# Second layer of the last MLP: seven block products for two token tiles instead of eight

## The chip, the cores and the metric

One core of a Trainium2 chip runs the program. Its engines are PE (TensorE, matrix products), DVE (VectorE), ACT (ScalarE), POOL (GpSimd) and SP, which here only issues DMAs. Each engine takes its instructions in program order; they wait for one another by semaphores. The metric is the device time of one execution in microseconds, the median of the runs shown; less is better.

## The reference, cut to what matters

Packed attention and a gated MLP give `x` of 4608 tokens with 512 features (the `y` of the kernel). The last part is

```
a = x @ w1            # 512 -> 1024
b = x @ w2            # 512 -> 1024
h = a * b @ w3        # 1024 -> 1024
out = h @ w_out       # 1024 -> 512
```

Everything is float32. The weights come as pairs of 32-bit words (64-bit floats) and are converted on the chip.

## The kernel before, in words

Tokens are cut into nine tiles of 512 (`TT`, `NTILE`). A float32 product is made of three fast ones: each operand is split into `hi` (ACT copies it into the reduced format, line 55) and `lo` (DVE or POOL subtracts, line 56), and PE adds hi·hi, hi·lo and lo·hi in one PSUM bank.

After the attention and the gate layer, the program goes through these stages:

- **`y_part(t)`** (line 538) makes `y` of one tile: 12 units, one for each row block `kk` of the hidden layer, of 12 matmuls each. `fetch_h` loads the row of a unit four units ahead into one of five buffers `hr`, `split_h` splits it two units ahead (three buffers `hh` and `hl`). At the end `y` is split into `y_h` and `y_l` and both go to DRAM three units later (`store_later`); tile 8 stays in SBUF.
- **`folded(half)`** (line 595) multiplies `w3` and `w_out` into `w34`, which goes to DRAM.
- **Conversion.** `converting` (line 116) loads a weight block of 512 KB some jobs ahead (`load64`), and `convert` needs two ACT, two DVE and one POOL instruction for it. `together` (line 405) takes steps of such generators between the units of the main one. The three calls at lines 613 to 616 are three `y` tiles with `folded(0)`, two with `folded(1)`, and the tiles 5, 6 and 7 with the last 15 jobs (the blocks of `w1` and `w2`, split into `w12_h`, `w12_l`, which stay in SBUF). `y_part(8)` comes last, with `last_loads`, which loads and splits `w34` in eight steps.
- **The layer itself**, tile by tile, in eight steps `i` of 128 features each. `ab_part(t, i)` (line 641) does two times 12 matmuls of 512 columns, for `a` and `b` in a PSUM bank each. ACT copies `a`, DVE multiplies by `b`, and the product is split. `out_part(t, i)` (line 659) does 12 matmuls into the four banks of the tile's output, one step later, so that PE has the next `ab_part` while the product is made. `fetch_y` loads the tile after next.

All DMAs are issued by SP in program order. A tile's buffers rotate: a load into a buffer waits until the last reader of its old content is done.

Of the kernel before, what the change touches and what calls it, by code (L numbers as in the profile page):

```python
# [32 lines left out]
def packed_attention_swiglu_bilinear(ctx: ExitStack, tc, qT, kT, v, pT, rms_g, w_gv, w_out,  # L33
# [11 lines left out]
    yh_d = dram.tile([NT // TT, 128, 4, TT], F32, name="yh_d")  # L45
    yl_d = dram.tile([NT // TT, 128, 4, TT], F32, name="yl_d")
# [69 lines left out]
    def converting(jobs, take):  # L116


        ahead = [load64(src) for src, *_ in jobs[:AHEAD64]]
        yield  # L120
        for i, job in enumerate(jobs):
            take(ahead.pop(0), *job[1:])
            if i + AHEAD64 < len(jobs):
                ahead.append(load64(jobs[i + AHEAD64][0]))
            yield
# [4 lines left out]
    def as_f32(w):  # L130
        o = cv_of[0].tile([128, 512], F32, tag="c_o", name="c_o", bufs=2)
# [3 lines left out]
    converted = set()  # L135

# [7 lines left out]
    AHEAD64 = 3  # L144
# [334 lines left out]
    wp = ctx.enter_context(tc.tile_pool(name="wo", bufs=1, side="left"))  # L479
# [57 lines left out]

    def y_part(t, tag):
# [13 lines left out]
        h = yp.tile([128, 4, TT], F32R, tag="y_h", name="y_h", bufs=2)  # L552
        l = yp.tile([128, 4, TT], F32R, tag="y_l", name="y_l", bufs=2)
        for m in range(4):
            split(h[:, m], l[:, m], acc[m], nc.vector)
        if t + 1 < NTILE:
            store_later(3, out=yh_d[t], in_=h.bitcast(F32))
            store_later(3, out=yl_d[t], in_=l.bitcast(F32))
        else:
            yt[t] = h, l  # L560
# [16 lines left out]

    jobs = []
# [16 lines left out]
    def folded(half, tag):  # L595
        acc = four(tag)
        ready(16 + 8 * half)
        for j in range(8):
# [16 lines left out]
    together(chained(y_part(3, "at"), y_part(4, "gv"), folded(1, "at")), 32.0, (8, some(late, 8), 0.0, 0.7))
    together(chained(y_part(5, "gv"), y_part(6, "at"), y_part(7, "gv")), 36.0, (15, late, 0.0, 0.95))
    split(*behind.pop(), nc.vector)
# [106 lines left out]
```

## Time and profile before

| | |
|---|---|
| time, median of 3 runs | 1469.1 us (1468.96 to 1470.85) |
| profiled execution: time, span of its core | 1469.47 us, 1467.7 us |
| PE busy | 1401.5 us, 95% of the span |
| DVE, ACT, POOL busy | 642.8, 539.7, 329.6 us |
| moved by DMA | 180.23 MB, mean 123 GB/s |
| PE waits after the start of the `y` stage | 1.4 us in all, both in `y_part(8)` |

PE is busy almost all the time, and from the `y` stage on it hardly waits. The other engines and the DMA queues have room on the average, least in the stage of the `y` tiles.

### The profile page before, as it was taken

What the parts mean: (1) busy time and instruction counts of PE and PEld (TensorE: products, weight loads), DVE (VectorE), ACT (ScalarE), POOL (GpSimd) and SP (SyncE); (2) the same over time, 40 slices, a digit from 0 to 9 for tenths busy, and PEclk for the clock granted to TensorE, in tenths of its full rate; (3) what the DMA queues carried; (4) which work ended last, traced back from release to release, by engine and by line L of the source; (5) the groups of instructions that cost most, each with busy time, mean ns of one, the idle gap of its engine ahead of it and who ended that gap; (6) DMA issues with size and microseconds to landing.
All of it is one profiled execution on the core that took longest, in us unless ns stands there. A gap on an engine that the chain in (4) does not pass through costs nothing.

```text
span 1467.7 us, 22283 instructions
## 1 busy us (share of the span) xinstructions
PE 1401.5 (95%) x8872; PEld 1150.7 (78%) x8872; DVE 642.8 (44%) x1088; ACT 539.7 (37%) x1079; POOL 329.6 (22%) x332
## 2 busy tenths in 40 slices
PE   3679999999999899999999999999999999999998
PEld 1468778778788788888888878888888888888887
DVE  4787576666666457726266531111111121111111
ACT  2455555555555555535255431111111111111111
POOL 2456445445445542201012220000000000000000
PEclk7599999999999999999999999999999999999999
DMA  9754453454222466746357620202020210202000
GB/s 303 279 203 126 155 181 115 148 162 139 79 88 88 160 240 238 250 172 213 132 186 262 232 94 0 86 1 87 0 86 0 87 60 27 86 1 86 0 29 29
DMA packets 59608, 180.23 MB, mean 123 GB/s; under 512 B 6768, under 2 KB 6768, under 8 KB 52720
## 3 DMA queue, kind: packets, MB, share of 16 engines
q1 hardware_dynamic: 59504, 178.81, 35.1%
q8 instruction: 69, 1.13, 0.3%
q14 instruction: 35, 0.29, 0.1%
HBM read 119.02 MB, written 59.77 MB: 122 GB/s over the span
## 4 chain that ended last, share of the span: by engine, by line
PE 85%; DVE 6%; ACT 3%; DMA 3%; issue 2%; POOL 0%; SPq 0%; ACTq 0%; DVEq 0%; POOLq 0%
PE gv L648 27%; PE gv L374 16%; PE at L663 14%; PE at L547 10%; PE gv L547 9%; PE at L335 2%; DMA w<-in_w_gv_dram 2%; PE at L601 1%; PE gv L601 1%; PE at L290 1%; DVE th L381 1%; DVE a L272 1%; PE at L206 1%; DVE wbl L56 1%; DVE wgv L112 1%
## 5 line engine op out<-in xcount | busy, mean ns | idle before, releaser
L653 DVE TENSOR_TENSOR hr<-hr,gv 128x512 f32<-128x512 f32 x72 | 49.5, 687 | 422.4 <-PE gv L648 422.4
L56 DVE TENSOR_TENSOR hl<-hr,hh 128x512 fp32r<-128x512 f32 x180 | 153.3, 855 | 182.7 <-ACT hh L55 162.8
L55 ACT ACTIVATE hh<-hr 128x512 fp32r<-128x512 f32 x180 | 112.8, 630 | 306.4 <-DVE hr L653 208.9
L386 POOL TENSOR_TENSOR ht<-th,vl 128x288 f32<-128x288 f32 x192 | 163.8, 861 | 178.4 <-ACT vl L385 97.7
L374 PE MATMUL gv<-ah,wbh 128*128 128x288 f32 x768 | 179.4, 315 | 16.0 <-ACT vl L385 12.5
L374 PEld LDWEIGHTS gv<-ah,wbh 128*128 128x128 f32 x768 | 123.3, 191 | 67.5 <-issue 26.9
L374 PE MATMUL gv<-al,wbh 128*128 128x288 f32 x768 | 167.3, 298 | 0.0
L374 PE MATMUL gv<-ah,wbl 128*128 128x288 f32 x768 | 165.6, 297 | 0.0
L648 PE MATMUL gv<-y_h,w_h 128*128 128x512 f32 x576 | 155.6, 392 | 0.0
L648 PE MATMUL gv<-y_l,w_h 128*128 128x512 f32 x576 | 155.4, 391 | 0.0
L648 PE MATMUL gv<-y_h,w_l 128*128 128x512 f32 x576 | 154.8, 391 | 0.0
L652 ACT ACTIVATE hr<-gv 128x512 f32<-128x512 f32 x72 | 43.1, 598 | 274.6 <-PE gv L648 274.6
L114 POOL TENSOR_TENSOR c_o<-c_o,c_y 128x512 int32<-128x512 int32 x52 | 73.1, 1406 | 248.8 <-DVE c_o L112 245.0
L648 PEld LDWEIGHTS gv<-y_l,w_h 128*128 128x128 f32 x576 | 108.1, 188 | 23.8
L648 PEld LDWEIGHTS gv<-y_h,w_h 128*128 128x128 f32 x576 | 108.1, 188 | 23.7
L648 PEld LDWEIGHTS gv<-y_h,w_l 128*128 128x128 f32 x576 | 108.1, 188 | 23.3
L374 PEld LDWEIGHTS gv<-al,wbh 128*128 128x128 f32 x768 | 125.4, 191 | 1.1 <-DVE al L56 0.6
L374 PEld LDWEIGHTS gv<-ah,wbl 128*128 128x128 f32 x768 | 124.8, 190 | 0.0
L663 PE MATMUL at<-w_h,hl 128*128 128x512 f32 x288 | 113.6, 395 | 0.0
L663 PE MATMUL at<-w_l,hh 128*128 128x512 f32 x288 | 113.3, 393 | 0.0
L663 PE MATMUL at<-w_h,hh 128*128 128x512 f32 x288 | 112.0, 389 | 0.0
L381 DVE SCALAR_TENSOR_TENSOR th<-th,gv 128x288 f32<-128x288 f32 x192 | 84.2, 444 | 63.1 <-ACT th L380 62.1
(112 smaller groups left out, 2158.1 us busy)
## 6 DMA issues: line engine op xcount, KB each, us to landing
hT_d<-ht SPq DMA_DIRECT2D x96, 288.0 KB, 2.5
hr<-hT_d SPq DMA_DIRECT2D x108, 256.0 KB, 4.1
w<-in_w_gv_dram SPq DMA_DIRECT2D x24, 512.0 KB, 7.8
w<-in_w_out_dram SPq DMA_DIRECT2D x20, 512.0 KB, 4.5
v<-in_v_dram SPq DMA_DIRECT2D x8, 1152.0 KB, 7.5
q<-in_qT_dram SPq DMA_DIRECT2D x8, 1152.0 KB, 6.9
out_dram<-hr SPq DMA_DIRECT2D x36, 256.0 KB, 2.1
w<-in_w3T_dram SPq DMA_DIRECT2D x16, 512.0 KB, 4.8
```

Source lines behind the costliest of these rows:

```text
L55: nc.scalar.activation(out=hi, in_=src, func=AF.Copy)
L56: eng_lo.tensor_tensor(out=lo, in0=src, in1=hi.bitcast(F32), op=ALU.subtract)
L114: nc.gpsimd.tensor_tensor(out=d, in0=d, in1=shape(y), op=ALU.add)
L335: nc.tensor.matmul(t[32 * c:32 * c + 32, e, :], lhsT=gP1T[64 * e:64 * e + 64, c, :], rhs=wgv[64 * e:64 * e + 64, c, :, 256 * g:256 * g + 256],
L374: nc.tensor.matmul(t[:, :HALF], lhsT=w[:, e, 256 * i + 128 * f:256 * i + 128 * f + 128], rhs=x[:, e, HALF * hf:HALF * hf + HALF], start=(n ...
L381: nc.vector.scalar_tensor_tensor(out=th, in0=th, scalar=1.0, in1=t[:, :HALF], op0=ALU.add, op1=ALU.mult)
L386: nc.gpsimd.tensor_tensor(out=ht[:, hf], in0=th, in1=vl, op=ALU.mult)
L547: nc.tensor.matmul(acc[m], lhsT=w[:, kk, 128 * m:128 * m + 128], rhs=x, start=(kk == 0 and a == 0), stop=(kk == NF - 1 and a == 2))
L648: nc.tensor.matmul(p[j], lhsT=w[:, kk, j, 128 * i:128 * i + 128], rhs=x[:, kk], start=(n == 0), stop=(n == 11))
L652: nc.scalar.activation(out=a, in_=p[0], func=AF.Copy)
L653: nc.vector.tensor_tensor(out=a, in0=a, in1=p[1], op=ALU.mult)
L663: nc.tensor.matmul(acc[m], lhsT=x[:, 128 * m:128 * m + 128], rhs=w[:, i], start=(i == 0 and n == 0), stop=(i == 7 and n == 2))
```

## The change

The second layer is taken for two tiles at a time, as a product of 2 by 2 blocks. The rows of `w1` and `w2` are halved (256 input features each), `w1` and `w2` are the two block rows of the result, and the two token tiles are its two block columns. Seven products of sums of blocks replace the eight products of blocks: `prod(bank, j, start)` is one of them, six matmuls (three fast products for each of two row blocks). Some of them are added on top of a bank whose earlier content an engine has read before.

- `layer2` converts the 16 weight blocks in four groups of four and `group` makes seven sums of each group, split into hi and lo (POOL and DVE; ACT for hi), in one of two SBUF tiles `stage`. They go to DRAM as `ws_d`, four stores of 917 KB for each group.
- `y` of a tile goes to DRAM unsplit, once (`y_d`, 1 MB instead of two times 1 MB); tile 8 too.
- For each pair of tiles `fetch_y` loads both `y`, and `sums` makes seven sums of their blocks and splits them (`xh`, `xl`, one buffer each). In each of the eight steps of a pair `load_w` loads the block sums of the next step from `ws_d`, 1.835 MB, into one of two buffers.
- The first tile's output is added up during the steps (`acc1`), the second tile's behind them (`acc2`), from its kept products `n2_h` and `n2_l`; the next pair's `sums` lie in that part.
- Tile 8 has no partner and is taken as two halves of 256 tokens.
- `w34` is split half in `y_part(8)`, half in the first four steps of the first pair (`rest`), where the load and the split of a row stand directly behind each other.

```diff
-    AHEAD64 = 3
+    ahead64 = [3]
...
+    stage = [p2.tile([128, 8192], F32R, name=f"stage{i}") for i in range(2)]
+    ahead64[0] = 2
+    c_o_bufs[0] = 4
...
-            split(h[:, m], l[:, m], acc[m], nc.vector)
-        if t + 1 < NTILE:
-            store_later(3, out=yh_d[t], in_=h.bitcast(F32))
-            store_later(3, out=yl_d[t], in_=l.bitcast(F32))
+            evict(y[:, m], acc[m], m)
+        store_later(3, out=y_d[t], in_=y)
...
+        put(3, a22, nc.vector)
+        nc.gpsimd.tensor_tensor(out=a22, in0=a21, in1=a22, op=ALU.add)
+        put(0, a11, nc.vector)
+        nc.gpsimd.tensor_tensor(out=a21, in0=a11, in1=a21, op=ALU.subtract)
+        yield
+        nc.gpsimd.tensor_tensor(out=a11, in0=a22, in1=a11, op=ALU.subtract)
+        put(1, a12, nc.vector)
+        put(4, a22, nc.vector)
+        yield
...
+        put(2, a12, nc.vector)
+        for i in range(4):
+            store_later(2 + i, out=ws_d[4 * c + i, :, r], in_=to[:, i].bitcast(F32))
...
-    together(chained(y_part(5, "gv"), y_part(6, "at"), y_part(7, "gv")), 36.0, (15, late, 0.0, 0.95))
+    together(chained(y_part(5, "gv"), y_part(6, "at"), y_part(7, "gv")), 36.0, (33, layer2(), 0.0, 0.97))
+    flush()
+    p2_ctx.close()
...
+    wt = ctx.enter_context(tc.tile_pool(name="wt", bufs=1, side="right"))
...
+    def load_w(n):
+        if n < 8 * len(pairs):
+            w = wt.tile([128, 2, 7, 2, 128], F32R, tag="w", name="w", bufs=2)
+            nc.sync.dma_start(out=w.bitcast(F32), in_=ws_d[n % 8])
...
+        put(0, b11, nc.vector)
+        yield
+        diff(b11, b12, b11)
+        put(4, b11, nc.vector)
+        yield
...
     fetch_y(0)
-    together(y_part(NTILE - 1, "at"), 12.0, (8, last_loads(), 0.0, 0.9))
+    load_w(0)
+    together(y_part(NTILE - 1, "at"), 12.0, (8, sums(0), 0.0, 0.85), (4, last_loads(0), 0.1, 0.9))
...
+        for i in range(8):
+            wi = ws.pop(8 * p + i)
+            load_w(8 * p + i + 1)
+            if i == 0:
+                fetch_y(p + 1)
+            ta, tb, tc_ = (bank()[:, :w] for _ in range(3))
...
+            prod(ta, 0, True)
+            nc.scalar.activation(out=p1, in_=ta, func=AF.Copy)
+            if second:
+                second()
+            prod(tb, 5, True)
+            dve(u2, tb, p1, ALU.add)
+            prod(tc_, 4, True)
+            prod(ta, 1, False)
+            prod(tb, 6, False)
+            u3 = tmp()[:, :w]
+            dve(u3, tb, p1, ALU.add)
+            dve(c22, tc_, u3, ALU.add)
+            if i > 0:
+                if i == 1:
+                    acc1 = four("at")
+                outs(acc1, i - 1, *n1.pop(i - 1), ms)
+            prod(tb, 3, False)
+            c21 = tmp()[:, :w]
+            dve(c21, tb, p1, ALU.add)
+            dve(c21, c21, ta, ALU.mult)
+            prod(tc_, 2, False)
+            dve(u2, tc_, u2, ALU.add)
+            nc.gpsimd.tensor_tensor(out=u2, in0=u2, in1=c22, op=ALU.mult)
...
+            split(hi[:, :w], lo[:, :w], c21, nc.vector)
...
+            if p == 0:
+                next(rest, None)
...
+        outs(acc2, 0, n2_h[:, 0], n2_l[:, 0], ms)
+        outs(acc1, 7, *n1.pop(7), ms)
+        for m in ms:
+            store(rows[0], acc1, m)
+        ahead = sums(p + 1)
...
+        for m in ms:
+            outs(acc2, 7, n2_h[:, 7], n2_l[:, 7], (m,))
+            store(rows[1], acc2, m)
```

What moves is seen best in the order of the instructions at three places. The first is PE in the layer itself. Before, one step of a tile: two banks `gv` of 12 matmuls each, and the beginning of the 12 matmuls of `out_part`.

```order
L648 MATMUL gv_12169<-y_h_11730,w12_h_6924 128x512 x4
L648 MATMUL gv_12169<-y_l_11731,w12_h_6924 128x512 x4
L648 MATMUL gv_12169<-y_h_11730,w12_l_6925 128x512 x4
L648 MATMUL gv_12170<-y_h_11730,w12_h_6924 128x512 x4
L648 MATMUL gv_12170<-y_l_11731,w12_h_6924 128x512 x4
L648 MATMUL gv_12170<-y_h_11730,w12_l_6925 128x512 x4
L663 MATMUL at_12106<-w34_h_9524,hh_12153 128x512
L663 MATMUL at_12106<-w34_l_9525,hh_12153 128x512
```

After, step 0 of the first pair, from its third product on: 9806 is the bank `tc_`, 9804 is `ta`, 9805 is `tb`.

```order
L799 MATMUL gv_9806<-xh_9560,w_9538 128x512 x2
L799 MATMUL gv_9806<-xl_9561,w_9538 128x512 x2
L799 MATMUL gv_9806<-xh_9560,w_9538 128x512 x2
L799 MATMUL gv_9804<-xh_9560,w_9538 128x512 x2
L799 MATMUL gv_9804<-xl_9561,w_9538 128x512 x2
L799 MATMUL gv_9804<-xh_9560,w_9538 128x512 x2
L799 MATMUL gv_9805<-xh_9560,w_9538 128x512 x2
L799 MATMUL gv_9805<-xl_9561,w_9538 128x512 x2
L799 MATMUL gv_9805<-xh_9560,w_9538 128x512 x4
L799 MATMUL gv_9805<-xl_9561,w_9538 128x512 x2
L799 MATMUL gv_9805<-xh_9560,w_9538 128x512 x2
L799 MATMUL gv_9806<-xh_9560,w_9538 128x512 x2
```

A product is six matmuls, and a bank comes back after one or two other products. In step 0 the products 6 and 3 stand directly behind each other in `tb` (the `x4` are the last two matmuls of the one and the first two of the other); in the other steps 12 matmuls of `outs` stand between them.

The second place is SP's queue where `y_part(7)` ends and `y_part(8)` begins (`hr<-hT_d` is a row for a unit, `hr<-w_d` a row of `w34`). Before:

```order
L485 DMA hr<-hT_d 128x512 [waits DMAHW7_49,DMAHW2_49,DVE_49]
L485 DMA hr<-hT_d 128x512 [waits DMAHW3_49,DVE_49]
L631 DMA y_h<-yh_d 128x2048
L632 DMA y_l<-yl_d 128x2048
L485 DMA hr<-hT_d 128x512 [waits DMAHW4_49,DVE_49]
L485 DMA hr<-w_d 128x512 [waits DMAHW5_49,DVE_49]
L485 DMA hr<-hT_d 128x512 [waits DMAHW6_49,DVE_49]
L485 DMA hr<-w_d 128x512 [waits DMAHW7_49,DVE_49]
L485 DMA hr<-hT_d 128x512 [waits DMAHW4_49,Pool_49]
L354 DMA yh_d<-y_h 128x2048 [waits DMAHW0_49]
L354 DMA yl_d<-y_l 128x2048 [waits DMAHW1_49]
```

After:

```order
L497 DMA hr<-hT_d 128x512 [waits DMAHW1_49,DVE_49]
L356 DMA ws_d<-stage_6939 128x1792 [waits DMAHW0_49,DVE_49]
L356 DMA ws_d<-stage_6939 128x1792
L356 DMA ws_d<-stage_6939 128x1792 [waits DMAHW2_49]
L356 DMA ws_d<-stage_6939 128x1792 [waits DMAHW3_49]
L356 DMA y_d<-y 128x2048 [waits DMAHW4_49,DVE_49,Activation_49]
L694 DMA yi<-y_d 128x2048 [waits DMAHW5_49]
L694 DMA yi<-y_d 128x2048 [waits DMAHW6_49]
L703 DMA w<-ws_d 128x3584 [waits DMAHW2_49,DMAHW1_49,DMAHW3_49,DMAHW0_49,DMAHW7_49,PE_49,Pool_49]
L497 DMA hr<-hT_d 128x512 x3
L497 DMA hr<-w_d 128x512 [waits DVE_49]
```

Between the row for the last unit that is loaded in `y_part(7)` and the next three rows there now stand the last group's four stores of block sums, the store of `y` of tile 7, two loads of `y` and the first load of block sums, which waits for the four stores (its buffer lies where `stage` lay). Before, two loads of `y` stood there.

The third place is SP's queue at the start of the first pair, after the last row of `y_part(8)`:

```order
L356 DMA y_d<-y 128x2048 [waits DVE_49]
L703 DMA w<-ws_d 128x3584
L694 DMA yi<-y_d 128x2048 [waits DMAHW6_49]
L694 DMA yi<-y_d 128x2048 [waits Pool_49]
L497 DMA hr<-w_d 128x512 [waits DMAHW1_49,DMAHW0_49]
L703 DMA w<-ws_d 128x3584 [waits PE_49]
```

The row of `w34` that the first step of `rest` loads and splits at once stands behind 5 MB of other transfers.

## Rows read from the trace of the kernel before

**Rows 1.** The page: busy time, share of the span and instructions of each engine.
```profile
PE 1401.5 (95%) x8872; PEld 1150.7 (78%) x8872; DVE 642.8 (44%) x1088; ACT 539.7 (37%) x1079; POOL 329.6 (22%) x332
```

**Rows 2.** The page: the chain that ended last, by engine.
```profile
PE 85%; DVE 6%; ACT 3%; DMA 3%; issue 2%; POOL 0%; SPq 0%; ACTq 0%; DVEq 0%; POOLq 0%
```

**Rows 3.** Stretches: busy time and count of each engine, granted clock, DMA share, GB/s.
```profile
900.00:1440.00 540.00, 540.00 (x2355) 441.72 (x2354) 100.00 (x146) 89.91 (x147) 0.00 (x0) 1.00 0.12 43
760.00:830.00 70.00, 70.00 (x310) 57.96 (x310) 47.57 (x67) 39.06 (x67) 15.96 (x11) 1.00 0.65 221
```

**Rows 4.** Groups of the second layer (868 to 1467): busy us, mean ns, idle before.
```profile
L648 PE MATMUL gv<-y_h,w_h 128*128 128x512 f32 x576 | 155.6, 392 | 0.0
L663 PE MATMUL at<-w_h,hl 128*128 128x512 f32 x288 | 113.6, 395 | 0.0
...
L653 DVE TENSOR_TENSOR hr<-hr,gv 128x512 f32<-128x512 f32 x72 | 49.5, 687 | 422.4 <-PE gv L648 422.4
L55 ACT ACTIVATE hh<-hr 128x512 fp32r<-128x512 f32 x72 | 45.5, 632 | 208.9 <-DVE hr L653 208.9
```

**Rows 5.** Timeline of PE: first and last matmuls of the second layer.
```profile
868.55 1.09 PE L648 MATMUL gv<-y_h,w_h 128*128 128x512 f32 x4
...
1462.94 0.39 PE L663 MATMUL at<-w_h,hl 128*128 128x512 f32 x1
```

**Rows 6.** Timeline of PE in the gate layer, matmuls of 288 columns.
```profile
299.83 0.43 PE L374 MATMUL gv<-al,wbh 128*128 128x288 f32 x2
...
300.90 0.42 PE L374 MATMUL gv<-ah,wbl 128*128 128x288 f32 x2
```

**Rows 7.** Timeline in the second layer: end of a bank's matmuls, and its reader.
```profile
1206.25 1.07 PE L648 MATMUL gv<-y_h,w_l 128*128 128x512 f32 x4
...
1207.36 0.60 ACT L652 ACTIVATE hr<-gv 128x512 f32<-128x512 f32 x1 [2.11 <-PE gv L648]
```

**Rows 8.** DMA issues: KB each, median us from issue to landing.
```profile
y_h<-yh_d SPq DMA_DIRECT2D x8, 1024.0 KB, 5.0
y_l<-yl_d SPq DMA_DIRECT2D x8, 1024.0 KB, 7.0
...
hr<-w_d SPq DMA_DIRECT2D x8, 256.0 KB, 3.0
```

**Rows 9.** Stretches with little but stores, mixed traffic, and loads (columns as before).
```profile
750.00:755.00 5.00, 5.00 (x24) 4.14 (x23) 3.53 (x6) 2.73 (x5) 1.28 (x1) 1.00 0.66 212
775.00:780.00 5.00, 5.00 (x24) 4.13 (x23) 3.77 (x7) 3.57 (x7) 1.59 (x1) 1.00 1.02 417
...
1206.40:1214.00 7.60, 7.60 (x35) 6.23 (x34) 1.38 (x2) 1.23 (x2) 0.00 (x0) 1.00 0.90 336
```

**Rows 10.** Timeline in `y_part(8)`, with the issues of SP.
```profile
839.49 1.12 SPq L485 DMA_DIRECT2D hr<-w_d  x1
...
847.03 0.63 ACT L55 ACTIVATE w_h<-hr 128x512 fp32r<-128x512 f32 x1 [6.72 <-DMA hr<-w_d]
...
848.24 0.50 PE L547 MATMUL at<-hh,wo_h 128*128 128x512 f32 x1 [0.54 <-ACT hh L55]
...
849.62 0.50 PE L547 MATMUL at<-hl,wo_h 128*128 128x512 f32 x1 [0.88 <-DVE hl L56]
```

**Rows 11.** Timeline in `y_part(8)`: a POOL and a DVE instruction at one time.
```profile
852.51 1.29 POOL L56 TENSOR_TENSOR w_l<-hr,w_h 128x512 fp32r<-128x512 f32 x1 [3.50 <-ACT w_h L55]
...
852.99 1.37 DVE L56 TENSOR_TENSOR hl<-hr,hh 128x512 fp32r<-128x512 f32 x1 [2.82 <-ACT hh L55]
```

**Rows 12.** Stretches around waits of PE (columns as before).
```profile
10.00:12.00 2.00, 0.00 (x0) 0.00 (x0) 1.35 (x4) 1.34 (x2) 0.00 (x0) 1.00 1.20 391
12.00:14.00 2.00, 1.08 (x6) 1.06 (x7) 0.00 (x0) 2.00 (x6) 0.00 (x0) 0.69 1.03 252
14.00:16.00 2.00, 1.69 (x8) 1.21 (x6) 1.74 (x4) 2.00 (x5) 0.61 (x1) 0.50 0.95 221
...
845.00:850.00 5.00, 3.58 (x15) 2.41 (x15) 1.78 (x2) 1.67 (x3) 1.28 (x1) 1.00 0.51 185
```

More of the change, by code (lines that the diff above doesn't have):

```diff
@@ L135, in packed_attention_swiglu_bilinear @@
     converted = set()
+    c_o_bufs = [2]
     def gv_weight(w, g, c):
@@ L611, in folded, with last_split @@
         yield 1.0
+    def last_split():
+        split(*behind.pop(), nc.vector)
+        staged.append(0)
+        yield
     together(chained(y_part(0, "at"), y_part(1, "gv"), y_part(2, "at"), folded(0, "gv")), 44.0,
              (18, some(late, 18), 0.0, 0.78))
-    together(chained(y_part(3, "at"), y_part(4, "gv"), folded(1, "at")), 32.0, (8, some(late, 8), 0.0, 0.7))
-    together(chained(y_part(5, "gv"), y_part(6, "at"), y_part(7, "gv")), 36.0, (15, late, 0.0, 0.95))
-    split(*behind.pop(), nc.vector)
@@ L618, in packed_attention_swiglu_bilinear @@
-    cv2_ctx.close()
-    wq = ctx.enter_context(tc.tile_pool(name="w34", bufs=1, side="left"))
-    w34_h = wq.tile([128, 8, DM], F32R, name="w34_h")
-    w34_l = wq.tile([128, 8, DM], F32R, name="w34_l")
-    def last_loads():
-        for kk in range(8):
-            split(w34_h[:, kk], w34_l[:, kk], fetch(w34_d[128 * kk:128 * kk + 128, :]), nc.gpsimd)
-            yield
-    def fetch_y(t):
-        h = yp.tile([128, 4, TT], F32R, tag="y_h", name="y_h", bufs=2)
-        l = yp.tile([128, 4, TT], F32R, tag="y_l", name="y_l", bufs=2)
-        nc.sync.dma_start(out=h.bitcast(F32), in_=yh_d[t])
-        nc.sync.dma_start(out=l.bitcast(F32), in_=yl_d[t])
-        yt[t] = h, l
+    late = chained(late, last_split())
@@ L659, in out_part, with tmp @@
-    def out_part(t, i, acc, ms=range(4)):
-        hi, lo = abt[t, i]
+    wo_ctx.close()
+    p3 = ctx.enter_context(tc.tile_pool(name="p3", bufs=1, side="left"))
+    n2_h = p3.tile([128, 8, TT], F32R, name="n2_h")
+    n2_l = p3.tile([128, 8, TT], F32R, name="n2_l")
+    for kk in range(4, 8):
+        w34_h[kk] = p3.tile([128, DM], F32R, name=f"w34_h{kk}")
+        w34_l[kk] = p3.tile([128, DM], F32R, name=f"w34_l{kk}")
+    rest = last_loads(1)
+    def tmp(tag="hr", bufs=5):
+        return (rot if tag == "hr" else p3).tile([128, TT], F32, tag=tag, name=tag, bufs=bufs)
@@ L693, in packed_attention_swiglu_bilinear @@
+    for p in range(len(pairs)):
+        run(p)
     man.close()
```

216 lines of the change are left out of this document (143 added, 73 removed).

## The prediction

> **What bounds the kernel now.** I read the page first: PE is busy for 95% of the span [rows 1] and makes 85% of the chain that ended last [rows 2], so time comes off where PE does less or waits less. Then stretches, to get what one matmul costs. In the second layer 540 us hold 2355 matmuls of 512 columns, **0.2293 us each**; in the `y` stage 70 us hold 310, 0.226 us each, or 2.71 us for a unit of 12 [rows 3]. PE is busy for the whole of both. The layer's matmuls begin at 868.55 and the last one starts at 1462.94 and takes 0.39 [rows 5], which is 594.8 us; 9 tiles x 8 steps x 36 matmuls x 0.2293 give 594.3. No matmul group of the layer has idle time before it [rows 4]. Nothing but the number and the width of matmuls sets this stage. DVE is 68% busy in the `y` stage (47.57 of 70 us) and 19% in the layer (100 of 540), and the DMA share is 0.65 and 0.12 [rows 3]: the work that the change adds lies partly where there is less room.
>
> **What the change takes away.** A pair needs 8 steps x 7 products x 6 matmuls + 2 x 8 x 12 of the output = 528 matmuls of 512 columns for 576. Four pairs: 2112 x 0.2293 = 484.3 us. Tile 8, in halves, needs 336 matmuls of 256 columns and 96 of 512. The narrow ones have no row; 288 columns take (300.90 - 299.83) / 8 = 0.134 us [rows 6], and the 224 columns up to 512 make 0.0955, so 32 fewer than 288 make about 0.120. That is 40.3 + 22.0 = 62.3. Together 546.6 for 594.3: **-47.7 us**. (Bounds of the narrow ones: 0.115 if the whole pitch scaled with columns, 0.134 if it didn't fall any more; -2 to +5 us.)
>
> **Banks that come back.** A product that is added on top must wait until DVE or ACT has read the bank. A reader starts when the last matmul ends, and PE could have gone on 0.39 - 0.23 = 0.16 earlier; with the 0.04 between an end (1207.32) and its reader (1207.36) [rows 7] and 0.69 for the DVE instruction [rows 4], the bank is free about 0.9 us after its product. Between most uses lie one or two products of 1.38 us, or 12 output matmuls of 2.75 us, and that covers it. Step 0 has no output matmuls between the products 6 and 3: 0.95 us in four pairs, 0.55 at half width: **+4.4**. If the cover of the other 35 steps were gone it would cost 35 x 0.95 = 33 us; DVE has 7 such instructions, 4.8 us, in a step of 12.4 (9.6 if all took the 1.37 us that one takes beside POOL [rows 11]), so it isn't.
>
> **The boundary before `y_part(8)`.** First what transfers cost. The two 1.05 MB loads of `y` land 5.0 and 7.0 us after issues that lie 0.4 apart [rows 8], and that stretch moves 336 GB/s at a share of 0.90, 0.373 MB/us at full share; stores go at 417 / 1.02, 0.41; mixed small traffic at 212 / 0.66, 0.32 [rows 9]. A lone 0.26 MB lands after 3.0 [rows 8], 2.3 of it not data. A queue is served in order: the row of `w34` issued at 839.49, behind the stores of `y`, reaches ACT at 847.03, and PE waits 0.54 + 0.88 us for the row split behind it [rows 10]. Now count from T, where PE would start `y_part(8)`. The last block sum is made two units before, T - 5.7. Four stores, 3.67 MB from T - 4.5 on: until T + 4.4. The store of `y`: until T + 7. Two loads of `y`: T + 12.6. The first block sums: T + 17.5. Only then the row for the fifth unit, issued behind all that, lands near T + 19; ACT 0.63 [rows 4] and DVE 0.69 later, at T + 20.2, it can be used, where PE is through with four units at T + 10.8. ACT also sits on the first `sums` until T + 11, which splits the fourth unit's row late, but that lies inside the same wait. 9.3 us, and 0.9 for DVE, whose `sums` (difference, split, difference) fill more than a unit afterwards, less the 1.4 us that the same place costs now: **+8.8**. PE then stands still twice for some 4 us. At the start, where PE has nothing to do at 10 to 12 and little after it, the granted clock is 0.69 and then 0.50 of full speed (0.50 is 1.2 of 2.4 GHz); after the 1.4 us of this place now it stays 1.00 [rows 12]. Four us as at 12 to 16 cost 1.6 us a wait, so 0 to 3.2; I take **+2**.
>
> A rule of the Trainium skill speaks against the change here, in "TensorE: Matmul & The Clock Gate", section "HAM oscillation — how this bites in real kernels": gaps of PE bring the clock down and the work behind each gap begins slow. By the first rows above that is 3.2, by the last 0.
>
> **The first pair.** The store of `y` of tile 8, the second block sums and two loads of `y` are 1.05, 1.83 and 2.1 MB; from about 2 us after the pair's start they run until 4.5, 9.4 and 15.0, and the row of `w34` behind them lands at 16.5. ACT waits for it, at the end of step 0; the copy of step 1's first bank is done at 17.8, and PE wants that bank at 14.7 (10.6 + three products): **+3.3**. The next rows are issued a step ahead of their use.
>
> **The stream of block sums.** 1.835 MB take 2.3 + 1.835 / 0.373 = 7.2 us from issue. A buffer comes free at the start of a step, so a full step of 54 x 0.2293 = 12.4 us hides it. In step 0 it is issued 1.5 us late, behind the last output stores, and lands at about 9.2, before 9.6 + 0.95. The half tiles have steps of 42 x 0.120 + 6 x 0.2293 = 6.4: 0.8 late six times, and 9.2 - 5.6 = 3.6 at the first: **+8.4**.
>
> By the Trainium skill, "DMA: Bandwidth & Descriptors", section "Anatomy of one DMA — SWDGE (gpsimd) path", a DMA costs 2.0 us and 1 us for each 436 KB; this load would take an estimated 6.2 us, less than the half step, and the sum would be some 6 us lower. The page fits another issuing path, and the stretch of loads above is slower than its rate, so the sum stays with the rows.
>
> **The units with block sums** (`y_part(5)` to `(7)`). DMA time by the rates above: 36 rows 29.5, 16 blocks of weights 26, three `y` 7.7, the 12 stores that fall in 27, together 90 of 97.6 us. Where a row, a block and a store fall in one unit, 0.8 + 1.6 + 2.2 stand against 2.7; unit by unit the backlog grows to about 9 us, three quarters through group 2's conversion. A row is asked for some four units before its split is due and six before PE, so this hides. DVE goes from 68% to some 88%: 13 more splits net of the `y` halves (about 9 us more) and POOL's 16 additions of 1.29, which slow what runs beside them [rows 11]. Cover is the two units that a split is ahead, 5.4 us. Bounds 0 and 16 (1 us in each of the 16 units of a group); near the small end, since PE has no wait at all there now: **+2**. The unsplit `y`, `last_split` and the two-ahead loads: nothing, hidden in ACT and DVE time that falls.
>
> **Sum:** -47.7 + 4.4 + 8.8 + 2 + 3.3 + 8.4 + 2 = -18.8. The profiled execution took 1469.47 (span 1467.7 and 1.8 around it), 0.4 over the median: about **1450 us**. The layer would take some 563 us and `y_part(8)` some 11 us more than its 32.5.
>
> **Rivals.**
> - *Transfers are quicker than I reckon.* The second load of `y` lands 2.0 us after the first, issued 0.4 later: 0.43 MB/us [rows 8]. Then half steps lack 0.2 us, the first 3, the boundary shrinks by 2, the first pair by 1.5, no clock is lost and the `y` units lose nothing: 12 us less, 1439. Against it is the stretch's mean rate [rows 9].
> - *DVE becomes the bound in the units with block sums.* For it: 68% now, 88% worked out, an in-order engine that waits for ACT and POOL within each group. A us in each group unit gives 1465. Against it: four units of a group are followed by four of conversion, which have less.
> - *Slower: the block sums come too slowly.* The lowest rate at a nearly full share is 221 / 0.95 = 0.23 MB/us [rows 12]. A load then takes 10.2 us: the half tile loses 21 more, each pair's first step 1.6, the boundary 6, and the time is 1484. From about 0.27 MB/us down the change costs more than it saves. For it: each pair's first loads run beside output stores and loads of `y`; against it: the rows of `y`, 8 KB long in each partition, went at 0.373, and these are 14 KB.
> - That PE doesn't do less can't be: the instructions are counted.
>
> **How the numbers follow.** The forecast has 0.52, quicker transfers 0.22, DVE 0.13, slow block sums 0.08, and 0.05 stays for something else at either side. Faster (by over 0.2%, 2.9 us, about what can be told from no change): the first two, most of the third and some of the rest, 0.85; the same 0.06; slower 0.09. The range reaches to the quick case and to the DVE case: 1436 to 1466.
>
> **What would show it.** 1344 matmuls of 512 and 336 of 256 columns at line 799, the first at 0.229 each; idle PE time of about 1 us in step 0 of each pair, released by DVE; one wait of 4 us or more, twice, in `y_part(8)`, released by ACT or DVE behind a row that came by DMA; a wait for ACT in step 1 of the first pair; waits for the load of block sums in the half tile alone. It is wrong if block sums hold PE in full steps, if the `y` units show waits of more than 5 us in all, or if `y_part(8)` takes under 36 us.

## The result, and the profile after

| | before | after |
|---|---|---|
| time, median of 4 runs | 1469.26 us | **1453.72 us** (1451.48 to 1457.4) |
| profiled execution: time, span | 1469.47, 1467.7 us | 1451.91, 1450.1 us |
| PE busy | 1401.5 us | 1360.0 us |

The ratio is 0.9895, 95% interval 0.987 to 0.9919: faster by about 1%, 3.7 us above the forecast time and well inside the range. The page of the changed kernel, first its busy times, then its chain by engine and by line, for [rows 1, 2]:

```profile
PE 1360.0 (94%) x8824; PEld 1121.8 (77%) x8824; DVE 795.9 (55%) x1267; ACT 546.7 (38%) x1080; POOL 489.9 (34%) x438
...
PE 75%; DVE 8%; DMA 5%; ACT 3%; issue 3%; POOL 1%; SPq 1%; ACTq 0%; DVEq 0%; POOLq 0%
PE gv L799 22%; PE gv L376 17%; PE at L566 8%; PE gv L772 7%; PE at L772 7%; PE gv L566 6%; PE at L337 2%; DMA hr<-w_d 2%; DMA w<-ws_d 2%; PE at L657 2%; PE gv L657 2%; DVE stage L56 1%; PE at L292 1%; DVE c_t L111 1%; DVE th L383 1%
```

PE is still the bound, and two DMAs with 2% each are now among the first lines of the chain, which weren't there before: the rows of `w34` and the loads of block sums. DVE and POOL are busy for 153 and 160 us more than before.

Stretches of the changed kernel (columns as in [rows 3]): the second layer, the `y` units with block sums, and three places behind waits of PE.

```profile
900.00:1370.00 470.00, 466.46 (x2033) 382.77 (x2034) 201.40 (x267) 93.34 (x140) 120.00 (x75) 1.00 0.40 148
760.00:830.00 70.00, 67.53 (x296) 55.29 (x297) 59.34 (x73) 41.10 (x72) 36.92 (x24) 1.00 0.94 349
...
1383.00:1393.00 10.00, 9.81 (x64) 9.56 (x65) 3.42 (x8) 1.75 (x5) 1.47 (x2) 0.83 0.49 182
850.00:855.00 5.00, 1.99 (x4) 1.29 (x5) 2.96 (x3) 1.66 (x3) 0.00 (x0) 0.58 1.04 441
...
901.00:906.00 5.00, 4.81 (x14) 3.86 (x15) 0.86 (x2) 0.66 (x2) 2.25 (x2) 0.66 0.37 153
```

The layer is dense: PE is idle for 3.5 of 470 us. In the `y` units it was busy for the whole 70 us before; now it lacks 2.5 us there, DVE has gone from 47.57 to 59.34 us and the DMA share from 0.65 to 0.94. In the last three rows the granted clock is below 1.00.

What PE waited for from the start of the `y` tiles to the end (total us, times, longest):

```profile
PE at L566 <- ACT hh L55: 7.3, 2, 6.7
PE gv L799 <- DMA w<-ws_d: 6.1, 4, 2.8
PE gv L799 <- DVE hr L767: 3.6, 5, 0.8
PE gv L799 <- ACT hr L805: 3.6, 1, 3.6
PE gv L566 <- DVE hl L56: 2.3, 3, 1.2
PE at L566 <- DVE hl L56: 2.1, 3, 1.3
```

25 us in all, for 1.4 before. Line by line: `y_part(8)`, the stream of block sums in the half tiles, the banks of step 0, the first pair, and in the last two lines the splits of the `y` units (3.6 us in `y_part(5)` to `(7)`, 0.8 in `y_part(8)`).

The stages, from the timeline of PE. What lies ahead of the first `y` tile is the same program in all kernels here, yet that tile begins at 527.4 to 532.1 us in them, so stages are compared and not ends:

| us | before | after | by |
|---|---|---|---|
| tiles 0 to 4 and `folded` twice | 207.52 | 206.92 | -0.6 |
| `y_part(5)` to `(7)` | 97.96 | 102.79 | +4.8 |
| `y_part(8)` | 34.61 | 44.78 | +10.2 |
| second layer | 594.78 | 564.06 | -30.7 |
| ahead of it all and behind it | | | -1.3 |

First and last matmul of the layer, for [rows 5] (the first and the last line). The two lines between are for [rows 6]: the first of 42 matmuls of 256 columns without a wait, and the matmul of 512 columns that follows them.

```profile
882.22 0.63 PE L799 MATMUL gv<-xh,w 128*128 128x512 f32 x2
...
1425.89 0.40 PE L799 MATMUL gv<-xh,w 128*128 128x256 f32 x2
...
1430.92 0.39 PE L772 MATMUL at<-w_h,hh 128*128 128x512 f32 x1
...
1445.89 0.39 PE L772 MATMUL gv<-w_h,n_l 128*128 128x512 f32 x1
```

42 narrow matmuls take 1430.92 - 1425.89 = 5.03 us, 0.120 each.

**The boundary**, for [rows 10]: the timeline of SP's issues, ACT and PE around the start of `y_part(8)` at 837.44.

```profile
834.44 3.01 SPq L356 DMA_DIRECT2D ws_d<-stage  x4
838.40 0.36 SPq L356 DMA_DIRECT2D y_d<-y  x1
838.80 2.54 SPq L694 DMA_DIRECT2D yi<-y_d  x2
844.78 0.32 SPq L703 DMA_DIRECT2D w<-ws_d  x1
845.15 2.10 SPq L497 DMA_DIRECT2D hr<-hT_d  x3
...
850.83 1.06 ACT L55 ACTIVATE xh<-yi 128x1024 fp32r<-128x1024 f32 x1 [12.56 <-DMA yi<-y_d]
851.80 0.61 ACT L55 ACTIVATE hh<-hr 128x512 fp32r<-128x512 f32 x1
...
858.32 0.63 ACT L55 ACTIVATE hh<-hr 128x512 fp32r<-128x512 f32 x1 [2.35 <-DMA hr<-hT_d]
...
852.46 0.80 PE L566 MATMUL at<-hh,wo_h 128*128 128x512 f32 x1 [6.70 <-ACT hh L55]
...
859.00 0.50 PE L566 MATMUL at<-hh,wo_h 128*128 128x512 f32 x1 [0.64 <-ACT hh L55]
```

Read from the last but one upwards: PE waits 6.70 us for the split of the fourth unit's row. ACT makes that split at 851.80, directly behind the first split of `sums`, and for that one it had stood still for 12.56 us, until the `y` of the pair was there, loaded behind four stores of block sums. The row itself had long been in SBUF: it was issued at 832.03, ahead of the stores. The fifth unit's row, issued at 845.15 behind all those DMAs, lands 13.1 us later and costs 0.64 us.

The whole of `y_part(8)`, and the half tiles (columns as in [rows 3]):

```profile
837.44:882.22 44.78, 36.45 (x146) 28.16 (x144) 23.15 (x21) 15.35 (x22) 9.72 (x5) 0.92 0.64 243
...
1374.44:1446.29 71.85, 65.23 (x433) 59.76 (x431) 28.42 (x58) 10.61 (x27) 11.76 (x16) 0.98 0.55 200
```

**First pair**, ACT and PE:

```profile
900.03 0.63 ACT L55 ACTIVATE w_h<-hr 128x512 fp32r<-128x512 f32 x1 [6.19 <-DMA hr<-w_d]
...
901.19 0.73 PE L799 MATMUL gv<-xh,w 128*128 128x512 f32 x2 [3.64 <-ACT hr L805]
```

**DMA**: KB each and median us from issue to landing, for [rows 8].

```profile
w<-ws_d SPq DMA_DIRECT2D x40, 1792.0 KB, 7.4
...
ws_d<-stage SPq DMA_DIRECT2D x16, 896.0 KB, 8.3
```

### The profile page after: what moved, and what is told of

The parts are those of the page before. It is cut to its first block, busy times and chain, and to the rows that moved or that the text cites. A ratio compares the mean times of both kernels' runs of the same rounds, so it can differ in the third digit from the quotient of the medians.

```text
span 1450.1 us, 22603 instructions
## 1 busy us (share of the span) xinstructions
PE 1360.0 (94%) x8824; PEld 1121.8 (77%) x8824; DVE 795.9 (55%) x1267; ACT 546.7 (38%) x1080; POOL 489.9 (34%) x438
## 4 chain that ended last, share of the span: by engine, by line
PE 75%; DVE 8%; DMA 5%; ACT 3%; issue 3%; POOL 1%; SPq 1%; ACTq 0%; DVEq 0%; POOLq 0%
PE gv L799 22%; PE gv L376 17%; PE at L566 8%; PE gv L772 7%; PE at L772 7%; PE gv L566 6%; PE at L337 2%; DMA hr<-w_d 2%; DMA w<-ws_d 2%; PE at L657 2%; PE gv L657 2%; DVE stage L56 1%; PE at L292 1%; DVE c_t L111 1%; DVE th L383 1%
## 5 line engine op out<-in xcount | busy, mean ns | idle before, releaser
L799 PE MATMUL gv<-xh,w 128*128 128x512 f32 (+1 forms) x1120 | 288.7, 373 | 13.5 <-DMA w<-ws_d 6.1
L55 ACT ACTIVATE hh<-hr 128x512 fp32r<-128x512 f32 (+1 forms) x148 | 91.2, 618 | 421.1 <-DVE hr L767 332.9
L799 PEld LDWEIGHTS gv<-xh,w 128*128 128x128 f32 x1120 | 201.9, 190 | 53.3 <-DMA w<-ws_d 7.4
L56 DVE TENSOR_TENSOR hl<-hr,hh 128x512 fp32r<-128x512 f32 (+1 forms) x148 | 140.4, 951 | 63.2 <-ACT hh L55 60.2
L799 PE MATMUL gv<-xl,w 128*128 128x512 f32 (+1 forms) x560 | 162.3, 372 | 0.0
L799 PEld LDWEIGHTS gv<-xl,w 128*128 128x128 f32 x560 | 102.6, 191 | 18.4
L566 PE MATMUL at<-hh,wo_h 128*128 128x512 f32 x240 | 94.7, 394 | 7.3 <-ACT hh L55 7.3
L387 ACT ACTIVATE vl<-gv 128x288 f32<-128x288 f32 x192 | 79.3, 413 | 58.5 <-PE gv L376 57.2
L566 PE MATMUL at<-hl,wo_h 128*128 128x512 f32 x240 | 94.8, 395 | 2.3 <-DVE hl L56 2.1
L382 ACT ACTIVATE th<-gv 128x288 f32<-128x288 f32 x192 | 79.4, 413 | 42.9 <-PE gv L376 42.9
```

What stands on the lines that cost most here:

```text
L55: nc.scalar.activation(out=hi, in_=src, func=AF.Copy)
L56: eng_lo.tensor_tensor(out=lo, in0=src, in1=hi.bitcast(F32), op=ALU.subtract)
L382: nc.scalar.activation(out=th, in_=t[:, :HALF], func=AF.Tanh, scale=0.5)
L387: nc.scalar.activation(out=vl, in_=t[:, :HALF], func=AF.Copy, scale=0.5)
L566: nc.tensor.matmul(acc[m], lhsT=w[:, kk, 128 * m:128 * m + 128], rhs=x, start=(kk == 0 and a == 0), stop=(kk == NF - 1 and a == 2))
L799: nc.tensor.matmul(t, lhsT=wi[:, r, j, a], rhs=x[b][:, j, r, :w], start=(start and n == 0), stop=(n == 5), skip_group_check=True)
```

## The experiments

Each kernel was timed beside the kernel before (1468.6 to 1471.1 us). The stages come from one profiled execution; the last column is the time from the first matmul of the `y` tiles to the last matmul of all, which is 934.9 us before. Of the medians only those of e7 to e11 are clear of the interval of the change; the others are told apart by their stages. A stage that no edit touches varies too: `y_part(8)` takes 44.8 to 46.6 us in after, e4, e5, e9 and e13, and the half tiles 71.4 to 73.5 in all kernels but e4 and e9. A difference of less than 2 us in one of these two says nothing.

| kernel | median us | ratio, interval | `y_part(5..7)` | `y_part(8)` | layer | from `y` on |
|---|---|---|---|---|---|---|
| after | 1453.7 | 0.9895, 0.987 to 0.9919 | 102.8 | 44.8 | 564.1 | 918.6 |
| e1 rows first | 1455.4 | 0.9901, 0.988 to 0.9922 | 103.0 | 46.9 | 564.8 | 921.6 |
| e2 sums late | 1456.8 | 0.9911, 0.9896 to 0.9926 | 102.2 | 48.6 | 562.1 | 919.8 |
| e3 both of these | 1459.7 | 0.9933, 0.9918 to 0.9948 | 102.3 | 50.4 | 563.7 | 923.3 |
| e4 both outputs | 1455.2 | 0.9896, 0.9879 to 0.9914 | 103.4 | 46.0 | 564.6 | 920.9 |
| e5 rest ahead | 1450.8 | 0.9868, 0.9853 to 0.9883 | 103.5 | 46.6 | 559.6 | 916.6 |
| e7 `y` ahead | 1447.0 | 0.9846, 0.9831 to 0.9861 | 102.7 | 36.7 | 567.1 | 913.4 |
| e8 no POOL sums | 1446.8 | 0.9841, 0.9819 to 0.9864 | 98.0 | 43.0 | 565.4 | 913.3 |
| e9 product twice | 1499.9 | 1.021, 1.0193 to 1.0227 | 102.4 | 45.9 | 609.4 | 964.6 |
| e10 e5 with e7 | 1442.8 | 0.9815, 0.9795 to 0.9835 | 102.7 | 36.6 | 561.5 | 907.7 |
| e11 e10 with e13 | **1437.0** | 0.9773, 0.9745 to 0.9801 | 99.3 | 36.4 | 562.2 | 904.8 |
| e13 sums on DVE | 1450.3 | 0.9871, 0.985 to 0.9892 | 98.4 | 45.9 | 563.8 | 914.9 |

**e1. Which load holds `y_part(8)`: the rows or the `y` of the pair?** The rows of units 4 to 6 are issued ahead of the stores.

```diff
+    for n in range(NF * 8 + 4, NF * 8 + 7):
+        fetch_h(n)
     flush()
```

> Only the rows of the units 4, 5 and 6 of the last y tile are loaded ahead of the block-sum stores. Theory A (the first and longer wait of PE there is ACT, which stands on the first sums until y has come back from DRAM behind 4.7 MB of stores; the row of unit 4 ends the second, short wait): the wait for ACT of 6.7 us at unit 3 stays, the wait at unit 4 (0.64 + 0.22) goes, the last y tile takes about 43.5 us for 44.8, the whole 1 us less. Theory B (as the prediction's ledger had it: the row of unit 4, last behind 8.65 MB, is what holds PE, and ACT's stand on the sums lies inside that wait): nearly all of it goes, the tile takes 36 us or less and the whole some 9 us less.

The wait for the fifth unit's row is gone and the fourth unit's is 3 us longer; ACT and PE there:

```profile
855.94 1.06 ACT L55 ACTIVATE xh<-yi 128x1024 fp32r<-128x1024 f32 x1 [15.54 <-DMA yi<-y_d]
...
857.57 0.80 PE L566 MATMUL at<-hh,wo_h 128*128 128x512 f32 x1 [9.68 <-ACT hh L55]
```

So the longer wait is ACT standing on `y`, and rows put ahead only push the stores and `y` back: SP issues the loads of `y` at 843.62, 4.0 us after the tile's start, for 1.4 in the changed kernel. The theory that the row alone holds PE falls, since ACT's stand is enough by itself; the other one had its gain wrong, since this edit gave none.

**e2. The sums later, so that ACT doesn't stand on them.**

```diff
-    together(y_part(NTILE - 1, "at"), 12.0, (8, sums(0), 0.0, 0.85), (4, last_loads(0), 0.1, 0.9))
+    together(y_part(NTILE - 1, "at"), 12.0, (8, sums(0), 0.45, 1.0), (4, last_loads(0), 0.1, 0.6))
```

> Only the first pair's sums begin later, from the middle of the last y tile on (45% instead of 0%), so that ACT doesn't stand on them; the order of the DMAs is unchanged. Theory A with two independent blocks: the wait at unit 3 goes, and one at unit 4 of some 10 us takes its place, since that row still lands 21 us after the tile's start and PE is through with four units after 10.9; the tile takes 44 to 47 us, the whole is not faster. Rival (the sums on ACT are all of it): the tile takes 36 us and the whole is 9 us faster.

The wait at the fourth unit goes and one at the fifth takes its place, as the first theory had it, but the tile takes 48.6 us, above its range. PE and ACT there:

```profile
861.79 0.63 ACT L55 ACTIVATE w_h<-hr 128x512 fp32r<-128x512 f32 x1 [18.58 <-DMA hr<-w_d]
...
862.99 0.80 PE L566 MATMUL at<-hh,wo_h 128*128 128x512 f32 x1 [12.29 <-ACT hh L55]
```

PE waits 12.29 us in one piece, until 23.3 us after the tile's start at 839.66. The fifth unit's row was issued at 847.42 and landed 13.0 us later, 20.8 us after the start; it is the block that the prediction counted. In the changed kernel PE starts on that row 0.8 us after it lands, so alone it would hold PE for some 10.5 us here, an estimate. The rest is ACT again: with the sums out of the way, the next instruction in its queue that needs a late load is the split of a `w34` row, and the fifth unit's split stands behind that. So not the sums or one row matter, but any instruction that needs a DMA issued behind the stores.

**e3. Both edits.**

> Both edits. If the two blocks are what holds PE, and only both together free it, the last y tile takes 35 to 38 us for 44.8 (the row of unit 7 may be 2 to 3 us late, it is still behind the first block sums), the clock isn't lowered there, and the whole is 7 to 10 us less than the changed kernel, about 1445. If something else holds the tile (DVE with the sums), it stays above 41 us.

Worse again (50.4 us, a wait of 14.14): the expectation failed. The rows of the units are ahead here and the sums late, and the split of the first `w34` row, which the edit left early, holds ACT and with it PE. So it shows a third block and says nothing of the two edits without it.

**e7. `y` of the pair loaded before the stores.** It is asked for while layer 2's first group is made, so that it lies in SBUF when `y_part(8)` starts; the rows are issued as in e1, sums and `w34` rows come later and at most two steps in a unit.

```diff
+            if g == 0:
+                fetch_y(0)
             yield from group(g)
...
-    together(y_part(NTILE - 1, "at"), 12.0, (8, sums(0), 0.0, 0.85), (4, last_loads(0), 0.1, 0.9))
+    together(y_part(NTILE - 1, "at"), 12.0, (8, sums(0), 0.3, 1.0), (4, last_loads(0), 0.5, 1.0), most=2)
```

> Everything that ACT or PE can stand on at the last y tile is taken from behind the stores: the first pair's y is loaded after the first group's conversion, the rows of units 4 to 6 ahead of the last stores of block sums, the first sums begin at 30% of the tile and the rows of w34 at 50%. Theory (an in-order engine standing on a transfer that is queued behind stores is all that holds PE there, whichever transfer it is): the tile takes 33 to 36 us for 44.8, the clock isn't lowered, and the whole is 8 to 11 us less than the changed kernel, about 1444. Rival (DVE's and ACT's work for the sums in fewer units holds PE instead): the tile stays above 38 us, with waits for DVE or ACT that themselves wait for no transfer. The 2.1 MB loaded earlier may cost up to 2 us in the y tiles before.

`y_part(8)` falls from 44.8 to 36.7 us, with 1.53 us as its longest wait and a granted clock of 1.00. The row of that wait, the tile, and the half tiles:

```profile
860.29 0.49 PE L566 MATMUL at<-hh,wo_h 128*128 128x512 f32 x1 [1.53 <-ACT hh L55]
...
839.56:876.22 36.66, 33.80 (x145) 26.79 (x144) 20.39 (x20) 14.36 (x22) 8.97 (x4) 1.00 0.68 251
...
1369.98:1443.35 73.37, 66.83 (x433) 61.28 (x431) 28.48 (x58) 10.61 (x27) 11.76 (x16) 0.95 0.54 196
```

This is the proof by removal: with no load behind the stores that ACT must wait for early, the boundary costs 2.0 us more than in the kernel before, not 10.2. It removes all three blocks at once (`y`, the rows, the early splits of `w34`), so what each is worth alone isn't shown; e1, e2 and e3 show only that any one of them left over holds PE. The tile is just above its range, and the whole gained 6.8 us instead of 8 to 11: the layer lost 3.1, half of it in the first pair, with a wait of 1.57 for block sums that are now loaded later, and half in the half tiles, which wait no longer than in the changed kernel but run longer at the lower clock (0.95 for 0.98). That half isn't the edit's doing: e10 has the same edit and takes 72.0 us there.

**e5. The first pair: the first of its four `w34` rows is loaded before the pair.**

```diff
-    rest = last_loads(1)
+    rest_x = [fetch(w34_d[512:640, :])]
+
+    def rest_steps():
+        for kk in range(4, 8):
+            split(w34_h[kk], w34_l[kk], rest_x.pop(0), nc.gpsimd)
+            if kk < 7:
+                rest_x.append(fetch(w34_d[128 * kk + 128:128 * kk + 256, :]))
+            yield
+
+    rest = rest_steps()
```

> In the first pair a row of w34 is loaded one step before its split, the first one ahead of the second block sums and the two loads of y. Theory (ACT stands on that row, which is behind 5 MB of other transfers): the wait for ACT of 3.6 us in step 1 of the first pair goes, with the lowered clock of 3.4 us behind it, the first pair takes about 122 us for 127.5 and the whole is 4 to 5 us less than the changed kernel. Rival (the load is only carried along, PE stands there because the second block sums land late, at 10 us or more after the pair's start): a wait of about 1 us or more for the load of block sums takes its place and less than half is gained.

The wait of 3.64 us for ACT is gone and a wait of 0.71 for block sums takes its place; the pair takes 122.6 us for 127.5 (from one step 0 to the next). `y_part(8)`, which the edit doesn't touch, came out 1.8 us longer in this execution, so that of 4.9 us only 1.9 are left from `y` on. The median fell by 2.9 us, less than the 4 to 5 expected.

**e4. The half tiles: both halves' outputs inside the steps, so that a step is longer than a load.**

```diff
                 outs(acc1, i - 1, *n1.pop(i - 1), ms)
+                if inside:
+                    outs(acc2, i - 1, n2_h[:, i - 1], n2_l[:, i - 1], ms)
```

> For the half tiles of tile 8 the output of the second half is added up in the steps too, 6 more matmuls of 512 columns in each: a step has 42 x 0.120 + 12 x 0.2285 = 7.8 us of PE instead of 6.4, and the number of matmuls is unchanged. Theory (a load of block sums takes 7.4 us from issue to landing, and waits come only where a step is shorter): the three waits for block sums in the later steps (1.56 + 0.59 + 1.16 = 3.3 us) go, the first (2.8, issued late behind the output stores) stays; the half tiles take about 68.5 us for 71.8, the whole 3 us less. Rival (the loads are late for another reason, the rate of the transfers at this place): the waits stay at 3 us or more.

Waits for block sums behind the first one fall from 3.3 to 0.6 us, so the mechanism holds. Nothing is gained: the half tiles take 72.3 us for 71.8, where 68.5 were expected. The last step's product and a copy of the output are now waited for at the end (0.70, 0.24 and 0.69 us), and the granted clock of these tiles is 0.95 for 0.98. Whether the edit lowers the clock isn't shown, as e7 has 0.95 there without it. The first wait stays, 2.74 us, as the expectation has it.

**e8 and e13. The `y` units: POOL's additions.** e8:

> Left out: the 16 additions and subtractions that POOL does on the weight blocks, so that the seven splits of a group split blocks instead of sums; all splits, loads and stores stay. Theory (the waits of the y tiles 5 to 7 come from DVE, whose instructions take 1.7 us instead of 0.69 beside POOL's): the waits of 3.6 us go or fall below 1 us, the three tiles take 98 to 99.5 us for 102.8, and the whole is 3 to 4 us less. Rival (the transfers, at a share of 0.84 and 1.0 for long stretches, make rows and blocks late): the waits stay within 1 us of 3.6.

The three tiles take 97.96 us, to the hundredth what they took before. The whole loss of 4.8 us comes with these 16 additions. The median fell by 6.9 us, more than expected: the last stores are issued earlier too, and `y_part(8)` takes 43.0 us. e13 keeps the additions and moves them to DVE:

```diff
-        nc.gpsimd.tensor_tensor(out=a22, in0=a21, in1=a22, op=ALU.add)
+        nc.vector.tensor_tensor(out=a22, in0=a21, in1=a22, op=ALU.add)
```

(and the other three of `group` likewise)

> The change with nothing but its 16 additions on weight blocks moved from POOL to DVE, so that POOL does nothing in a group's units. Theory P (contention between the two engines): y_part(5) to (7) 98 to 100 us for 102.8, all DVE splits there 0.69 us, about 1449 to 1451 us in all. Theory Q (amount of DVE work): 106 to 111 us, 1457 to 1462. In the run without POOL's additions the three tiles took 98.0 us; that run can't tell P from Q, since it also took work away.

The timelines of POOL and DVE in the first group, in the changed kernel:

```profile
752.48 1.67 POOL L608 TENSOR_TENSOR c_o<-c_o 128x512 f32<-128x512 f32 x1 [1.47 <-DVE stage L56]
...
752.91 1.78 DVE L56 TENSOR_TENSOR hl<-hr,hh 128x512 fp32r<-128x512 f32 x1
754.62 3.48 DVE L56 TENSOR_TENSOR stage<-c_o,stage 128x512 fp32r<-128x512 f32 x2
```

and DVE in e13 at the same place:

```profile
752.09 0.69 DVE L608 TENSOR_TENSOR c_o<-c_o 128x512 f32<-128x512 f32 x1
752.70 0.68 DVE L56 TENSOR_TENSOR stage<-c_o,stage 128x512 fp32r<-128x512 f32 x1
```

The stretch of the three tiles, in e13 and then in the changed kernel:

```profile
734.32:832.67 98.35, 98.25 (x433) 81.02 (x432) 79.66 (x119) 59.33 (x103) 24.23 (x16) 1.00 0.88 320
```

```profile
734.65:837.44 102.79, 99.18 (x433) 80.81 (x432) 85.17 (x103) 59.75 (x103) 50.41 (x32) 1.00 0.84 306
```

A split beside a POOL addition takes 1.78 us; with the additions on DVE it takes 0.68 to 0.69. DVE with 16 more instructions is busy for 5.5 us less (79.66 for 85.17), and PE is idle for 0.1 us (98.35 less 98.25) where it was for 3.6. The three tiles and the median (98.4 and 1450.3) are those of the first theory; the second had the tiles at 106 or more. It is contention of the two engines, not the amount of work on DVE, and not a wait of one for the other either: in neither kernel does DVE wait for POOL in these tiles. The Trainium skill says in "Perfetto Trace Analysis", section "Optimizing Scalar/DVE Operations", that GpSimd and DVE share a read port of SBUF, so moving work between the two might not help. These rows agree, though no run shows the port itself: an addition on POOL makes a split on DVE 1.09 us longer, and on DVE it would take 0.69.

**e9. What the eighth product would cost.** One product of the seven is done twice.

```diff
             prod(tc_, 2, False)
+            prod(tc_, 2, False)
```

> The last of the seven products of each step is added a second time into its bank, so PE does eight products as a plain product of blocks would, with everything else the same (its value is wrong for that). Theory (in the layer PE is the bound, and the gain is the removed matmuls): 32 x 6 x 0.2285 = 43.9 us more for the full steps, and 5.8 for the half steps less the 3 us by which their waits for block sums shrink: the layer takes about 610 us for 564, the whole 46 to 48 us more than the changed kernel, about 1500, slower than before. Rival (DVE, POOL and the stream of block sums pace the steps, PE has slack): under 35 us more.

The layer is 45.3 us longer: 10.9 in each full pair (48 x 0.2265), less in the first pair and the half tiles, where it fills time in which PE waited. So the gain from the seven products is real, and of the size worked out; the whole is 46.2 us more, as expected.

**e10 and e11. The parts that helped, together.** e10 is e5 and e7, e11 has e13's edit too.

> The two edits that each measured faster than the change, put together: y of the first pair loaded while layer 2's first group is made, rows of units 4 to 6 ahead of the flush, sums and w34 rows of the first half later (as in the run with y ahead), and the first w34 row of the second half fetched before the pair (as in the run with the rest ahead). If the two waits are separate: y_part(8) 36.7 us, the first pair 122.5 to 124 us in place of 128.9, the other stages unchanged, 1441 to 1443.5 us, 3.5 to 6 under the run with y ahead. Rival: the wait of 1.57 us for block sums, which the run with y ahead has in its first pair, grows because one more row now stands ahead of that load; then 2 us of the gain are given back and the time is 1444.5 to 1446.

> As the combined kernel, and the 16 additions on weight blocks go from POOL to DVE. Theory P (contention): DVE's splits take 1.78 us for 0.69 beside POOL's additions, so a group loses some 4.4 us of DVE to them and pays only 4 x 0.69 = 2.8 for doing them itself; the three y tiles before the last take 98 to 100 us in place of 102.8 and the whole 1437 to 1441 us. Theory Q (amount of work): DVE is late because it has too much to do in a group unit, and 2.8 us more in each group lengthen the waits; the three y tiles take 106 to 111 us and the whole 1445 to 1451.

Both came out as the first theory had it. In e10 `y_part(8)` takes 36.6 and the first pair 123.9 us; the wait for block sums that its rival names has grown from 1.57 to 1.99 us only, with one of 0.55 in the second pair. The median falls by 10.9 us, for 2.9 and 6.8 of the two edits alone, which is the sum of the two within the intervals. e11 is the fastest version of the study: 1437.0 us, 16.7 under the change. What PE waits for in e11 from the `y` tiles on:

```profile
PE gv L811 <- DMA w<-ws_d: 8.5, 5, 3.2
PE gv L811 <- DVE hr L779: 3.7, 5, 0.8
PE at L566 <- DVE hl L56: 1.5, 2, 1.2
PE at L566 <- ACT hh L55: 1.2, 1, 1.2
PE gv L566 <- DVE hl L56: 0.6, 1, 0.6
```

What is left is the stream of block sums, 6.5 of the 8.5 us in the half tiles. A third buffer for it wasn't tried.

## Why the prediction was right, point by point

The sum came to -18.8 us and the span is 17.6 shorter. That the two lie so close is in part luck: three terms were 6.1 us too small, and the others, with what wasn't forecast, 5.0 too large. Term by term:

| term | forecast | measured | how |
|---|---|---|---|
| matmuls | -47.7 | -49.4 | 4 x (121.57 - 0.78) + 62.2 = 545.4 for 594.8 |
| banks in step 0 | +4.4 | +3.6 | 4 x 0.78 + 0.52 |
| boundary with its clock | +8.8 +2 | +10.2 | 44.78 - 34.61 |
| first pair | +3.3 | +5.9 | 127.50 - 121.57 |
| stream in half tiles | +8.4 | +9.1 | 71.84 - 62.2 - 0.52 |
| `y` units | +2 | +4.8 | 102.79 - 97.96 |
| not forecast | 0 | -1.9 | ahead, tiles 0 to 4, behind |

- **Matmuls.** 54 of them take 12.34 us in a full step, 0.2285 each for the forecast 0.2293; the narrow ones 0.120, as worked out. The later pairs take 121.57 us each. e9 confirms the price of a product from the other side.
- **Banks.** 0.78 us at each step 0 and 0.52 at half width, released by DVE, and none elsewhere: the cover named for the other steps held.
- **Boundary.** The size was right and the story half wrong. What was wrong is "ACT also sits on the first `sums` until T + 11, which splits the fourth unit's row late, but that lies inside the same wait". ACT's stand, until T + 13.4, is the first and by far the longest wait (6.70 us), and the sign named, a wait of 4 us or more twice, didn't come. The fifth unit's row, usable at T + 20.2 by the forecast, lets PE start at T + 21.6 and costs only 0.64 + 0.22, because PE starts the fourth unit late and at a lower clock. Each of the two alone holds PE about as long: e1 has the row in time and ACT's stand, e2 has no early sums and waits for the row, and neither gains. So the end that the count of arrivals gave stands, and taking out the block that it named wouldn't have helped. The "some 11 us more than its 32.5" fits the sum badly: the place took 34.61 us before, waits included, and took 44.78.
- **Its clock.** All waits of `y_part(8)` are 8.1 us. 144 matmuls take 32.65 at full clock (97.96 / 3), so 44.78 - 32.65 - 8.1 leaves 4.0 us for matmuls at the lower clock and restarts, against 2. The granted clock is 0.92 over the tile and 0.58 in the stretch of the wait; 0.50 is 1.2 of 2.4 GHz. The rule of the Trainium skill that the prediction weighed ("TensorE: Matmul & The Clock Gate", section "HAM oscillation — how this bites in real kernels") is borne out by these gaps: the work behind them begins slow. It isn't behind every gap (last section).
- **First pair.** Mechanism right, size short: 3.64 us of wait, and 2.3 at a clock of 0.66 behind it, which the forecast had left out here. e5 shows the mechanism: with the row in time that wait is gone.
- **Stream.** 6.1 us of waits and some 3 of lower clock, for 8.4 of waits alone; full steps hide it, as said. A load lands after 7.4 us, forecast 7.2. By "DMA: Bandwidth & Descriptors" of the Trainium skill, section "Anatomy of one DMA — SWDGE (gpsimd) path", the estimate was 6.2; the measurement decides, and the half steps do wait.
- **`y` units.** The term that was mis-sized: +2 of bounds 0 to 16. DVE is busy for 83% (85.17 of 102.79), not 88%, and PE waits four times, 3.6 us in all. The rows named [rows 11] showed the mechanism, a DVE instruction that takes 1.37 us beside one of POOL, for 0.69 alone; it was priced as one of several small things, near the small end of the bounds because PE had no wait there before. e8 and e13 show that it is the whole of it.

The rival of quicker transfers didn't come: a load of block sums lands after 7.4 us, more than a half step. Slow block sums didn't either: no full step waits for them. The rival of DVE as the bound came in small, 4.8 us and not 16.

## What to carry to other kernels

When a stage's inputs are written and read back just ahead of it, look at which in-order engine first meets a load that stands behind the stores: everything in that engine's queue waits with it. Moving one load forward, or one user back, gave nothing here, because the next one held PE as long; asking for all of the early ones before the stores, and starting the users of the rest later, gave 8 us. A product form with fewer matmuls is worth its count of matmuls where PE is dense, and what it costs is found at the stage's edges, one wait each. Additions "for free" on an idle POOL are not free where DVE is busy: try them on DVE.

## What the runs showed of the hardware that was not expected

- A DVE subtraction of 128 x 512 takes 1.78 us beside a POOL addition that takes 1.67, and 0.69 without one. Worked out from these, four such splits cost DVE 7.1 us (4 x 1.78); the same four and the four additions, all on DVE, 5.5 (8 x 0.69).
- Behind PE's idle times of 2.79 (half tiles), 3.64 (first pair) and 6.70 us the granted clock was 0.83, 0.66 and 0.58 over the stretches shown, and each such place cost 2 to 4 us on top of the wait. In e10 it stayed 1.00 around 1.47 us of idle time in `y_part(8)` and 1.99 in the first pair:

```profile
855.00:865.00 10.00, 8.30 (x36) 6.33 (x35) 5.40 (x6) 3.92 (x7) 2.19 (x1) 1.00 0.70 254
885.00:892.00 7.00, 5.01 (x22) 3.80 (x21) 3.05 (x5) 2.26 (x4) 3.56 (x3) 1.00 1.00 427
```

  So taking a wait away gave back more than its length: in e7 the waits of `y_part(8)` fell by 5.3 us and its time by 8.1.
- The part of the program that is the same in all kernels took 527.4 to 532.1 us until the first `y` tile.
